# Storing a spectral product channel by channel in a long-convolution kernel

## The chip, the cores and the metric

The kernel runs on one core of a Trainium2 chip. What counts is the device time of one execution in microseconds (us), as the median of several runs. Times below are in us unless marked ns. The engines are PE (TensorE: weight loads and matrix products), DVE (VectorE), ACT (ScalarE), POOL (GpSimd) and SP (SyncE, which here only issues DMAs). Each engine works through its own list of instructions in order.

## The reference

The input is one sequence of 2048 positions with 640 channels. After a layer norm it feeds two branches whose product is added back to the input:

```python
xn = _layernorm(x)
# branch A: a state-space convolution, one long kernel K per channel
P = exp((A * dt)[:, :, None] * pos)              # 640 channels x 128 modes x 2048 positions
K = 2 * einsum("dn,dnl->dl", C, P).real          # 640 kernels of 2048 taps
y = irfft(rfft(u, 2L) * rfft(K, 2L), 2L)[:L]     # causal convolution, plus u * D_skip
# branch B: a router picks 8 tokens for a gated expert; the others pass unchanged
g = silu(B(xn))
return x + s * g
```

## The kernel before

The 640 channels are 160 groups of four, worked on in **five batches of 32 groups** (`SIZES`). A sequence of 2048 positions is seen as 32 x 64, and its transform is done in two steps. For every batch the kernel does this:

1. **Kernel tables.** For four groups at a time PE forms phases (`arg`, L1030), ACT takes sines (L1044), POOL and DVE multiply them with magnitudes (L1007, L1016, L1051 to L1065), and PE sums over the 128 modes (`K`, L1078).
2. **First step of the transform.** Over the 32: `stage1_x` (L1122) transforms the signal, `stage1` (L1113) the kernel. The result has 32 residues for each channel, so a group has 4 x 32 = 128 values m. Their constants are `c[:, C_X...]` and `c[:, C_W...]`, built by `shape_constants()`. ACT and DVE copy the results out of PSUM (helper `copy`, L477) into `g_all` for the signal and `fk` for the kernel. `fk` holds 4096 floats in each partition; rows 0 to 63 belong to groups 0 to 15 of the batch and rows 64 to 127 to groups 16 to 31.
3. **Second step, product.** `dft` (L1151) runs for each of eight values `kp`, two halves each, on signal and kernel at once. `ue` copies one part out of PSUM (L477), `xp` multiplies (DVE, L1170), and `combine` makes the real and the imaginary part of the complex product with one subtraction and one addition (helper `tt`, L480; 34 of the 40 pairs on POOL, 6 on DVE). Its result goes back into `fk`, into the very places that this `kp` has just read.
4. **Inverse of the second step.** `inv` (L1193) runs four times a batch, for q = 0 to 3. Each time PE loads 32 stationary operands of 64 rows by 128 columns out of `fk` and multiplies each with 128 columns of the constants at `C_D`. Loads for rows 0 to 63 and rows 64 to 127 alternate, so 32 products are 16 pairs. One stationary operand is one group: its 128 columns are the 128 values m of that group's real or imaginary part. `inve` copies the result out of PSUM into `gb` (L477, 32 of the 40 copies on ACT, 8 on DVE).
5. **Last step and gate.** L1242 for the first three batches, L1332 for the last two, with the gate, the residual and the stores around them.

In `fk` the product lies as `(q r m g)`: half, real or imaginary, m, and then eight groups side by side. So the 128 columns that one `inv` loads stand **eight floats (32 bytes) apart**.

**What sets the order.** Nothing is decided while the kernel runs. A planner (`Plan`) holds all tasks; a table `ORDER` gives each its rank, and `CHOICE` gives the engine where there is a choice. The code is issued in the order of these ranks, so the tables of the next batch stand between the `inv` tasks of this one: on PE an `arg`, a `K` or a `stage1_x` that stands behind an `inv` cannot start before it. `inv` and most other products take their PSUM from one ring of four slots (`f`); an `inv` takes two. The layout also appears in the planner's bookkeeping: `stage1` for quarter q of `fk` waits for two `inv` tasks (`fkfree`).

Of the kernel before, what the change touches and what calls it, by code (L numbers as in the profile page):

```python
# [15 lines left out]
OP = mybir.AluOpType  # L16
# [125 lines left out]
}  # L142
MODE = {"K": 1, "rt": 1, "ff": 1, "t2m": 1, "s2": 2, "turn": 2, "inv": 3, "arg": 3, "s1x": 2, "s1k": 4, "t1m": 4, "t2g": 5}
CODE = {"K": 136, "s1x": 64, "s1k": 128, "rt": 128, "s2": 32, "inv": 64, "t1m": 64, "t2m": 64, "turn": 32, "ff": 20, "arg": 8, "t2g": 8}
BLOCK, FETCH, SHARE, CAP, SOFT = 254.9, 3.0, 1.0, 4.5, 1.3
SWITCH = 0.135
LETTER = {"PE": "P", "DVE": "D", "ACT": "A", "POOL": "G", "SP": "S"}
# [35 lines left out]
def shape_constants():  # L183
    bm = np.arange(64)
    k1, a, k2 = np.arange(32), np.arange(32), np.arange(64)
    c = np.zeros((128, C_END))
    w = np.zeros((4, 32, 2, 4, 32))
    ph = 2 * np.pi * (((4 * k1[None] + 1) * a[:, None]) % 128) / 128
    for d in range(4):
        w[d, :, 0, d] = np.cos(ph)  # L190
        w[d, :, 1, d] = np.sin(ph)
    c[:, C_X:C_X + 256] = w.transpose(0, 1, 2, 3, 4).reshape(128, 256)
    w = w.reshape(2, 64, 2, 2, 64)
    c[:, C_W:C_W + 128] = np.concatenate([w[0, :, :, 0], w[1, :, :, 1]]).reshape(128, 128)
# [12 lines left out]
    m[0, :, :, 0], m[1, :, :, 0] = np.cos(ph), -np.sin(ph)
    m[0, :, :, 1], m[1, :, :, 1] = np.sin(ph), np.cos(ph)
    l = 64 * a[None] + bm[:, None]
    ph = 2 * np.pi * (((4 * k1[:, None, None] + 1) * l[None]) % 8192) / 8192  # L210
    v = np.stack([np.cos(ph), np.sin(ph)], 2) / 2048.0
    v = np.broadcast_to(v[None], (4, 32, 64, 2, 32)).reshape(128, 64, 2, 32)

    pos = np.zeros((3, 2, 32))
    pos[0, 1], pos[1, 0], pos[2, 0] = (a + 0.5) / TURN, a / TURN, 1.0 / TURN
    p = np.zeros((4, 32, 2, 2, 4, 32))
    for q in range(4):
        for x in range(2):  # L220
# [194 lines left out]
def kernel(ctx: ExitStack, tc: tile.TileContext, xq, xp, xr, par, ldtp, dsk, wr, wg, wu, wd,  # L415
# [571 lines left out]
    def kernel(gg):  # L987
# [103 lines left out]
        if odd:  # L1091
            P.add(KEVAC, lambda e: copy(e, kb.t.rearrange("p e b -> p (e b)"), kp.t), [kp], [("kb", gg)], [kb], kind="kb")
            p, q = (Slot("f"), Slot("f")), (gg % 8) // 2
            free = [("fkfree", 2 * (q // 2) + z) for z in range(2)]
            on("PE", S1K, lambda: stage1(p, lambda e: kb.t[:, e]),
               [kb, ("kb", gg), "c"] + free, new=p, kind="s1k")
            for h in range(2):
                P.add(EVAC, lambda e, h=h: copy(e, fk[:, 1024 * q + 512 * h:1024 * q + 512 * h + 512].rearrange("p (m c) -> p m c", c=8),
                                                p[h].t.rearrange("p (c m) -> p m c", c=8)),
                      [p[h]] + free, [("fk", batch(gg), q, h)], kind="s1ke")  # L1100
# [41 lines left out]

    def dft(o, bi, kp, j):

        u = g_all[:, 4 * bi:4 * bi + 4].rearrange("p (s q) (d k i g) -> p s i k (q d) g", s=2, d=4, k=8, i=4)
        for e in range(2):
            for ri in range(2):
                for h in range(2):
# [2 lines left out]
                    T.matmul(o[64 * h:64 * h + 64, :, ri, e], ms[kp].t[:, 2 * j + e, 64 * ri:64 * ri + 64], v, start=True, stop=True,  # L1151
                             tile_position=(0, 64 * h))

    def transform(bi):
        udep = [("g", gg, h) for gg in range(STARTS[bi] // 4, (STARTS[bi] + NG) // 4) if gg % 2 == 0 for h in range(2)]
        kdep = [("fk", bi, q, h) for q in range(4) for h in range(2)]
        for kp in range(8):
            pq = Slot("pq")
            for j in range(2):
                p = Slot("f")  # L1160
                on("PE", S2, lambda p=p, kp=kp, j=j: dft(p.t.rearrange("p (a r x e g) -> p a r e x g", a=2, r=2, x=8, e=2), bi, kp, j),
                   [ms[kp]] + udep + kdep, [("S2", bi, kp, j)], [p], kind="s2", mac=.853)
# [11 lines left out]
                on("DVE", .62, product, [p, pq, ("u", bi, kp, j)], [("xp", bi, kp, j)], kind="xp")  # L1174

            def combine(e, pq=pq, kp=kp):
                z = fk.rearrange("p (q r d k x) -> p k r q d x", r=2, q=2, d=4, k=8)[:, kp]
                v = lambda k, u: pq.t[:, k, u].rearrange("p (q d x) -> p q d x", q=2, d=4)
                tt(e, z[:, 0], v(0, 0), v(1, 1), OP.subtract)
                tt(e, z[:, 1], v(1, 0), v(0, 1), OP.add)  # L1180

# [2 lines left out]
        for q in range(4):  # L1184
            p = Slot("f"), Slot("f")

            def inv(p=p, q=q):
                fz = fk.rearrange("p (q r m g) -> p r q g m", r=2, q=2, g=8)
                for j in range(4):
                    for ri in range(2):  # L1190
                        for h in range(2):
                            r = slice(64 * h, 64 * h + 64)
                            T.matmul(p[h].t[:, 128 * j:128 * j + 128], fz[r, ri, q // 2, 4 * (q % 2) + j],  # L1193
                                     c[r, C_D + 128 * ri:C_D + 128 * ri + 128], start=(ri == 0), stop=(ri == 1),
                                     tile_position=(64 * h, 0))
# [232 lines left out]
```

## Time and profile before

| | us |
|---|---|
| median of 3 runs (441.22 to 441.88) | 441.74 |
| the profiled execution | 442.32 |
| its span, first to last instruction | 440.4 |
| PE busy | 361.3 |
| DVE busy | 343.5 |
| POOL busy | 280.9 |
| ACT busy | 267.8 |
| mean granted PE clock | 0.961 |

"PE" is time in matrix products and "PEld" time in weight loads; the two overlap. A group of instructions is written as line, engine, operation, output<-input, shapes and count, then busy time and mean ns of one, then the idle time of the engine just before them and what ended it. Shapes of PE instructions begin with rows*columns of the stationary operand. The chain is the sequence of work that ended last, followed back from the last instruction; `154.00 3.80 PE f L1193 x32` means that from 154.00 on 32 instructions of line 1193 held the chain for 3.80 us. A timeline row has start, length, engine, line, operation and count, and in brackets how long the engine stood idle before and for what. A row of stages gives busy time and instruction count of PE, PEld, DVE, ACT and POOL in a stretch, then the PE clock, the DMA share and GB/s.

### The profile page before, as it was taken

What the parts mean: (1) busy time and instruction counts of PE and PEld (TensorE: products, weight loads), DVE (VectorE), ACT (ScalarE), POOL (GpSimd) and SP (SyncE); (2) the same over time, 40 slices, a digit from 0 to 9 for tenths busy, and PEclk for the clock granted to TensorE, in tenths of its full rate; (3) what the DMA queues carried; (4) which work ended last, traced back from release to release, by engine and by line L of the source; (5) the groups of instructions that cost most, each with busy time, mean ns of one, the idle gap of its engine ahead of it and who ended that gap; (6) DMA issues with size and microseconds to landing.
All of it is one profiled execution on the core that took longest, in us unless ns stands there. A gap on an engine that the chain in (4) does not pass through costs nothing.

```text
span 440.4 us, 19524 instructions
## 1 busy us (share of the span) xinstructions
PE 361.3 (82%) x8634; PEld 313.3 (71%) x8634; DVE 343.5 (78%) x665; ACT 267.8 (61%) x508; POOL 280.9 (64%) x345
## 2 busy tenths in 40 slices
PE   1066367866699996989899999999889899989995
PEld 1055356634477884867788899997688789889995
DVE  3787798999878947789977778558979987788255
ACT  3994936687648457567735486559866856541010
POOL 0558991655367858659653579738998974968200
PEclk9996859989999999999997999999999999999999
DMA  7915332649344411312101000303455651168704
GB/s 244 365 29 101 96 119 70 213 155 247 119 147 166 133 52 56 102 51 76 52 1 40 3 3 3 104 2 124 151 184 169 217 176 60 54 162 190 226 25 170
DMA packets 41596, 51.30 MB, mean 116 GB/s; under 512 B 19560, under 2 KB 30632, under 8 KB 41384
## 3 DMA queue, kind: packets, MB, share of 16 engines
q1 hardware_dynamic: 40200, 48.17, 36.0%
q10 hardware_dynamic: 1152, 1.84, 1.1%
q8 instruction: 68, 1.11, 1.0%
q14 instruction: 16, 0.13, 0.1%
q0 software_dynamic: 160, 0.04, 0.0%
HBM read 44.75 MB, written 10.52 MB: 125 GB/s over the span
## 4 chain that ended last, share of the span: by engine, by line
PE 45%; DVE 13%; ACT 5%; issue 3%; DMA 1%; POOL 1%; ACTq 0%; DVEq 0%; SPq 0%
PE f L1193 18%; PE f L1151 10%; DVE tab L1051 4%; PE f L1078 4%; PE f L1332 3%; PE f L1122 2%; PE pr L1030 2%; DVE both L1170 2%; PE f L1113 2%; ACT pr L1044 2%; ACT both L477 2%; PE f L1242 1%; DVE both L480 1%; DMA wflat<-cw 1%; DVE tab L1060 1%
## 5 line engine op out<-in xcount | busy, mean ns | idle before, releaser
L477 ACT COPY both<-f 128x512 f32<-128x512 f32 (+1 forms) x142 | 69.3, 511 | 100.4 <-PE f L1193 56.1
L1051 DVE TENSOR_TENSOR tab<-pr,ma 128x1024 f32<-128x1024 f32 x80 | 97.2, 1218 | 24.5 <-ACT pr L1044 15.3
L1007 POOL TENSOR_TENSOR ma<-ma,et 128x64 f32<-128x64 f32 (+4 forms) x100 | 89.6, 896 | 22.2 <-ACT ma L477 9.0
L1044 ACT ACTIVATE pr<-pr 128x1024 f32<-128x1024 f32 x80 | 80.4, 1014 | 30.3 <-PE pr L1030 28.2
L1193 PE MATMUL f<-c,both 64*128 64x128 f32 x640 | 80.4, 404 | 1.3 <-ACT both L477 1.1
L1193 PEld LDWEIGHTS f<-c,both 64*128 64x128 f32 x640 | 78.0, 331 | 3.0 <-issue 1.3
L1151 PE MATMUL f<-both 128*64 128x128 f32 x1280 | 76.3, 275 | 4.0 <-DVE both L1170 1.6
L1151 PEld LDWEIGHTS f<-both 128*64 128x64 f32 x1280 | 69.7, 137 | 10.5 <-DVE both L1170 3.9
L1065 POOL TENSOR_TENSOR tab<-tab,ma 128x256 f32<-128x256 f32 x48 | 34.9, 749 | 46.2 <-DVE tab L1051 44.6
L480 POOL TENSOR_TENSOR both<-both 128x256 f32<-128x256 f32 (+1 forms) x69 | 49.9, 748 | 15.6 <-DVE both L1170 12.6
L1170 DVE TENSOR_TENSOR both<-both,f 128x512 f32<-128x512 f32 x80 | 52.8, 683 | 3.9 <-ACT both L477 2.9
L477 DVE COPY both<-f 128x512 f32<-128x512 f32 (+1 forms) x58 | 32.1, 557 | 28.5 <-PE f L1193 20.6
L1078 PE MATMUL f<-tab 128*32 128x64 f32 x2560 | 45.6, 223 | 6.5 <-ACT both L477 2.4
L1078 PEld LDWEIGHTS f<-tab 128*32 128x32 f32 x2560 | 39.0, 111 | 16.0 <-issue 6.9
L1122 PE MATMUL f<-c,both 128*64 128x128 f32 x640 | 41.1, 282 | 2.4 <-ACT both L477 1.3
L1122 PEld LDWEIGHTS f<-c,both 128*64 128x64 f32 x640 | 36.3, 140 | 5.8 <-ACT both L477 2.2
L1016 POOL TENSOR_TENSOR ma<-ma,et 128x1024 f32<-128x1024 f32 x20 | 38.8, 1941 | 1.6
L1030 PE MATMUL pr<-pos,st 64*128 64x256 f16 x320 | 30.2, 282 | 10.2 <-DVE tab L1058 5.1
L1030 PEld LDWEIGHTS <-st 64*128 64x128 f16 x320 | 13.3, 101 | 22.0 <-issue 10.1
L1113 PE MATMUL f<-c,kb 64*64 64x64 f32 x1280 | 24.2, 221 | 4.1 <-issue 1.4
L1060 DVE SCALAR_TENSOR_TENSOR tab<-pr,ma 128x512 f32<-128x512 f32 x40 | 27.2, 679 | 0.0
L1113 PEld LDWEIGHTS f<-c,kb 64*64 64x64 f32 x1280 | 21.3, 134 | 7.8 <-issue 2.8
(170 smaller groups left out, 510.6 us busy)
## 6 DMA issues: line engine op xcount, KB each, us to landing
both<-xq SPq DMA_DIRECT2D x8, 640.0 KB
wflat<-wg SPq DMA_DIRECT2D x10, 432.0 KB
wflat<-wu SPq DMA_DIRECT2D x10, 432.0 KB
wflat<-wd SPq DMA_DIRECT2D x16, 270.0 KB
wflat<-cw SPq DMA_DIRECT2D x16, 256.0 KB
xg_d<-xp SPq DMA_DIRECT2D x4, 768.0 KB
wflat<-xg_d SPq DMA_DIRECT2D x16, 192.0 KB
ios<-xp SPq DMA_DIRECT2D x16, 192.0 KB
```

The lines of the kernel that those rows point to most:

```text
L477: {"ACT": S.copy, "DVE": V.tensor_copy, "POOL": G.tensor_copy}[e](out, in_)
L480: {"DVE": V, "POOL": G}[e].tensor_tensor(out, a, b, op=op)
L1007: G.tensor_tensor(both_at(m, 32 - 2 * w, w, w), both_at(m, 32 - w, 0, w), e()[:, q::6].unsqueeze(3).broadcast_to([128, 2, 32, w]), op=OP.mult)
L1030: T.matmul(o.t[:, j].rearrange("p (t h m) -> p h t m", t=2, h=2)[:, h], st.t[64 * j:64 * j + 64, 2 * (gg % 8) + h], pos[64 * j:64 * j + 64 ...
L1044: on("ACT", .93, lambda src=src: S.activation(src.t, src.t, AF.Sin, scale=-TWO_PI), [], [src], table="TS", kind="sin")
L1051: V.tensor_tensor(o, src.t.rearrange("p j (t x) -> p j t x", t=2), m, op=OP.mult)
L1078: T.matmul(o[32 * d4:32 * d4 + 32, dl, :], tab[i].t[:, 0, cc, :], tab[i].t[:, 1:3, cc], start=(not odd and dl + i == 0), stop=False, tile_ ...
L1113: T.matmul(p[h].t[64 * ri:64 * ri + 64, 64 * e:64 * e + 64], src(e)[64 * h:64 * h + 64], c[64 * h:64 * h + 64, w:w + 64], start=True, stop ...
L1122: T.matmul(p[e // 4].t[64 * ri:64 * ri + 64, 128 * (e % 4):128 * (e % 4) + 128], g_all[:, g0 // 8, 64 * e:64 * e + 64], c[:, C_X + 128 * r ...
L1151: T.matmul(o[64 * h:64 * h + 64, :, ri, e], ms[kp].t[:, 2 * j + e, 64 * ri:64 * ri + 64], v, start=True, stop=True, tile_position=(0, 64 * h))
L1170: V.tensor_tensor(bass.AP(tensor=o.tensor, offset=o.offset, ap=[o.ap[0], [512, 2], [32, 16], [1, 16]]), bass.AP(tensor=o.tensor, offset=o. ...
L1193: T.matmul(p[h].t[:, 128 * j:128 * j + 128], fz[r, ri, q // 2, 4 * (q % 2) + j], c[r, C_D + 128 * ri:C_D + 128 * ri + 128], start=(ri == 0 ...
```

## The change

The 32 columns of the first step's constants are permuted: the column that held residue 4k+i at place 4k+i now stands at place 8i+k. The second step finds each `kp` under the new index; its moving operand still has runs of eight floats 256 floats apart, at another offset.

With that, the eight floats that one `kp` writes back at each place are (i, real or imaginary) of **one** group and no longer eight groups. `combine` writes its result as `(g x k i r)`: m and, inside it, real and imaginary part, so that one group (the program's words "channel by channel") fills 256 consecutive floats and a stationary operand of `inv` takes every second one (8 bytes apart). To do so `combine` walks over 4 x 8 x 8 elements, reading runs of eight floats; the elements of its innermost loop go to places 512 floats (2 KB) apart. Before, it wrote runs of 32 floats.

Each `inv` then reads one quarter of `fk` (4q to 4q+3), so `stage1` is listed behind one `inv` in place of two. `inve` writes pairs of floats where it wrote runs of four; it reads the same PSUM addresses in the same order.

The list `APART` is empty, so the new functions `dft1`, `in_u`, `spectrum` and `second` are never called, and the loop in `transform` runs as before. Compared row by row, all five engines issue as many instructions as before, of the same operations and in the same order. PE's and SP's rows are equal. Only the shapes of `combine` (128x2x4x32 becomes 128x4x8x8) and `inve` (128x128x4 becomes 128x128x2x2) differ, and two ACT copies of `stage1` results no longer wait for POOL.

```diff
@@ shape_constants
+    w = w[..., np.arange(32).reshape(8, 4).T.ravel()]
-    c[:, C_X:C_X + 256] = w.transpose(0, 1, 2, 3, 4).reshape(128, 256)
+    c[:, C_X:C_X + 256] = w.reshape(128, 256)
...
@@ kernel
-            free = [("fkfree", 2 * (q // 2) + z) for z in range(2)]
+            free = [("fkfree", q)]
...
@@ dft
-        u = g_all[:, 4 * bi:4 * bi + 4].rearrange("p (s q) (d k i g) -> p s i k (q d) g", s=2, d=4, k=8, i=4)
+        u = g_all[:, 4 * bi:4 * bi + 4].rearrange("p (s q) (d i k g) -> p s i k (q d) g", s=2, d=4, k=8, i=4)
...
@@ transform, combine
-                z = fk.rearrange("p (q r d k x) -> p k r q d x", r=2, q=2, d=4, k=8)[:, kp]
-                v = lambda k, u: pq.t[:, k, u].rearrange("p (q d x) -> p q d x", q=2, d=4)
+                z = fk.rearrange("p (g x k i r) -> p k r i x g", g=8, x=8, k=8, r=2)[:, kp]
+                v = lambda k, u: pq.t[:, k, u].rearrange("p (x i g) -> p i x g", x=8, i=4)
...
@@ transform, inv
-                fz = fk.rearrange("p (q r m g) -> p r q g m", r=2, q=2, g=8)
+                fz = fk.rearrange("p (h m r) -> p h m r", h=HALF, r=2)
...
-                            T.matmul(p[h].t[:, 128 * j:128 * j + 128], fz[r, ri, q // 2, 4 * (q % 2) + j],
+                            T.matmul(p[h].t[:, 128 * j:128 * j + 128], fz[r, 4 * q + 2 * (j % 2) + j // 2, :, ri],
...
@@ transform, inve
-                g = HALF * h + 4 * q
-                P.add(EVAC, lambda e, p=p[h], g=g: copy(
-                    e, gb[:, bi].rearrange("p (m g) -> p m g", g=NG)[:, :, g:g + 4], p.t.rearrange("p (g m) -> p m g", g=4)),
+                P.add(EVAC, lambda e, p=p[h], q=q, h=h: copy(
+                    e, gb[:, bi].rearrange("p (m s u g) -> p s m u g", s=2, u=2, g=8)[:, h, :, :, 2 * q:2 * q + 2],
+                    p.t.rearrange("p (u g m) -> p m u g", u=2, g=2)),
```

More of the change, by code (lines that the diff above doesn't have):

```diff
@@ L142 @@
 }
-MODE = {"K": 1, "rt": 1, "ff": 1, "t2m": 1, "s2": 2, "turn": 2, "inv": 3, "arg": 3, "s1x": 2, "s1k": 4, "t1m": 4, "t2g": 5}
-CODE = {"K": 136, "s1x": 64, "s1k": 128, "rt": 128, "s2": 32, "inv": 64, "t1m": 64, "t2m": 64, "turn": 32, "ff": 20, "arg": 8, "t2g": 8}
+MODE = {"K": 1, "rt": 1, "ff": 1, "t2m": 1, "s2": 2, "s2u": 2, "s2k": 2, "turn": 2, "inv": 3, "arg": 3, "s1x": 2, "s1k": 4, "t1m": 4, "t2g": 5}
+CODE = {"K": 136, "s1x": 64, "s1k": 128, "rt": 128, "s2": 32, "s2u": 64, "s2k": 64, "inv": 64, "t1m": 64, "t2m": 64, "turn": 32, "ff": 20, "arg": 8, "t2g": 8}
 BLOCK, FETCH, SHARE, CAP, SOFT = 254.9, 3.0, 1.0, 4.5, 1.3
@@ L161 @@
 S2 = .93
+APART = []
 S1K, S1X = 1.1, 1.9
@@ L1152, in dft, with dft1, in_u, spectrum @@
                              tile_position=(0, 64 * h))
+    def dft1(p, bi, kp, src):
+        o = p.t.rearrange("p (r x i g) -> p r i x g", r=2, x=8, i=4)
+        v = src.rearrange("p (s q) (d i k g) -> p s i k (q d) g", s=2, d=4, k=8, i=4)
+        for e in range(4):
+            for ri in range(2):
+                for h in range(2):
+                    T.matmul(o[64 * h:64 * h + 64, ri, e], ms[kp].t[:, e, 64 * ri:64 * ri + 64], v[:, h, e, kp], start=True, stop=True,
+                             tile_position=(0, 64 * h))
+    def in_u(bi, kp):
+        return g_all[:, 4 * bi:4 * bi + 4].rearrange("p q (x k g) -> p k (q x) g", x=16, k=8)[:, kp]
+    def spectrum(bi):
+        udep = [("g", gg, h) for gg in range(STARTS[bi] // 4, (STARTS[bi] + NG) // 4) if gg % 2 == 0 for h in range(2)]
+        for kp in range(8):
+            p = Slot("f")
+            P.chain(("u", kp), on("PE", 1.0, lambda p=p, kp=kp: dft1(p, bi, kp, g_all[:, 4 * bi:4 * bi + 4]),
+                                  [ms[kp]] + udep, [("U", bi, kp)], [p], kind="s2u", mac=.853), 8 * STEP)
+            P.add(EVAC, lambda e, p=p, kp=kp: copy(e, in_u(bi, kp), p.t.rearrange("p (x g) -> p x g", g=8)),
+                  [p] + udep, [("X", bi, kp)], kind="s2ue")
+    def second(bi, kp, pq, kdep):
+        p = Slot("f")
+        on("PE", .95, lambda: dft1(p, bi, kp, fk.rearrange("p (q y) -> p q y", q=4)), [ms[kp]] + kdep, [("S2", bi, kp, j) for j in range(2)],
+           [p], kind="s2k", mac=.853)
+        def product():
+            u, v = in_u(bi, kp), p.t
+            V.tensor_tensor(pq.t.rearrange("p k u x -> p (k u x)"),
+                            bass.AP(tensor=u.tensor, offset=u.offset, ap=[u.ap[0], [0, 2], list(u.ap[1]), list(u.ap[2])]),
+                            bass.AP(tensor=v.tensor, offset=v.offset, ap=[v.ap[0], [256, 2], [0, 2], [1, 256]]), op=OP.mult)
+        on("DVE", 1.135, product, [p, ("X", bi, kp)], [("xp", bi, kp, j) for j in range(2)], [pq], kind="xp")
     def transform(bi):
@@ L1158, in transform @@
             pq = Slot("pq")
-            for j in range(2):
+            if bi in APART:
+                second(bi, kp, pq, kdep)
+            for j in range(2 * (bi not in APART)):
                 p = Slot("f")
@@ L1377 @@
         P.chain(("s", gg % 8), stage1_x(gg), 8 * STEP)
+        if gg % 8 == 6 and batch(gg) in APART:
+            spectrum(batch(gg))
     for bi in range(NBATCH):
```

## The prediction

> **What bounds the kernel now.** First the page: who is busy, and who holds the chain that ended last.
>
> ```profile
> PE 361.3 (82%) x8634; PEld 313.3 (71%) x8634; DVE 343.5 (78%) x665; ACT 267.8 (61%) x508; POOL 280.9 (64%) x345
> ...
> PE 45%; DVE 13%; ACT 5%; issue 3%; DMA 1%; POOL 1%; ACTq 0%; DVEq 0%; SPq 0%
> PE f L1193 18%; PE f L1151 10%; DVE tab L1051 4%; PE f L1078 4%; PE f L1332 3%; PE f L1122 2%; PE pr L1030 2%; DVE both L1170 2%; PE f L1113 2%; ACT pr L1044 2%; ACT both L477 2%; PE f L1242 1%; DVE both L480 1%; DMA wflat<-cw 1%; DVE tab L1060 1%
> ```
>
> PE leads, but DVE is close behind. One line stands out: the inverse, L1193, holds 18% of the chain. Then the chain in order of time, which tells whether that is a few long waits or every `inv`:
>
> ```profile
> 154.00 3.80 PE f L1193 x32
> ...
> 227.15 4.21 PE f L1193 x32
> ...
> 253.49 1.90 PE f L1122 x32
> ...
> 410.34 15.43 PE f L1193 x128
> ```
>
> All 20 `inv` tasks are on it, 3.8 us each at full clock (4.2 at 227, in a stage whose mean clock is 0.90, row below). Between them stands the yardstick: L1122 also makes 32 products in 16 pairs, also streams 128 columns and also fills the array, but needs **1.90**. The groups say what differs:
>
> ```profile
> L1193 PE MATMUL f<-c,both 64*128 64x128 f32 x640 | 80.4, 404 | 1.3 <-ACT both L477 1.1
> L1193 PEld LDWEIGHTS f<-c,both 64*128 64x128 f32 x640 | 78.0, 331 | 3.0 <-issue 1.3 <-ACT both L477 1.1
> ...
> L1122 PE MATMUL f<-c,both 128*64 128x128 f32 x640 | 41.1, 282 | 2.4 <-ACT both L477 1.3 <-ACT st L477 0.8 <-DVE both L812 0.2
> L1122 PEld LDWEIGHTS f<-c,both 128*64 128x64 f32 x640 | 36.3, 140 | 5.8 <-ACT both L477 2.2 <-issue 1.3 <-ACT st L477 1.1
> ```
>
> In L1193 weight loads are under way 78.0 of 80.4 us. A load there has 128 columns in place of 64, so twice the work, but 331 ns is more than twice 140. For a load of 128 columns that stand side by side there is the layer norm's sum over constants:
>
> ```profile
> 30.56 0.52 PEld L781 LDWEIGHTS f<-wflat,c 128*128 128x128 f32 x4 [3.02 <-ACT wflat L775]
> L781 PEld LDWEIGHTS f<-wflat,c x8: 186/240/333, 30.6 to 33.0; 128*128 128x128 f32 x8
> ```
>
> Four loads there end 0.52 after the first began, the last of them taking about 0.19: they start (0.52 - 0.19) / 3 = **0.11** apart. In L1193 a pair of loads, which run side by side on the two halves of the rows, comes every 15.43 / 64 = **0.241**. So 128 columns cost 0.11 side by side and 0.241 at 32 bytes apart, and the products need no more than 1.90 / 16 = 0.119 a pair. The inverse waits for its weight loads, and the loads for the spacing.
>
> **The change part by part.**
>
> *Weight loads 8 bytes apart.* No row has this spacing. Bounds: the loads stay at 0.241 (`inv` 3.8, no gain), or they fall to or below the pace of the products (0.119, `inv` 1.90). I take 0.120. Why: at 32 bytes every column is fetched by itself, 0.241 / 128 = 1.9 ns each, against 0.11 / 128 = 0.86 side by side. If a fetch brings a block of 16 bytes or more, two columns or more now share one, and 128 columns need at most 0.241 / 2 = 0.120. An `inv` then takes 16 x 0.120 = 1.92, **1.89 less** than 3.81; twenty of them 37.8.
>
> [...]
>
> *How much of 37.8 reaches the end.* Behind an `inv` PE's list holds `arg` (L1030) and `K` (L1078), for which ACT's sines and DVE's tables wait. What comes earlier by a faster `inv` is their work, so the next bound is DVE. The stages with `inv`, and for comparison the one where DVE rules:
>
> ```profile
> 154.00:164.00 10.00, 10.00 (x150) 9.02 (x148) 4.14 (x6) 5.52 (x8) 6.41 (x6) 1.00 0.19 58
> 179.00:189.00 10.00, 9.95 (x144) 8.89 (x142) 5.83 (x12) 4.58 (x8) 7.75 (x8) 1.00 0.19 58
> 189.00:227.00 38.00, 33.20 (x826) 26.98 (x824) 36.73 (x66) 25.70 (x49) 27.10 (x33) 1.00 0.17 52
> 227.00:262.00 35.00, 33.89 (x746) 31.08 (x748) 25.16 (x48) 19.80 (x35) 18.46 (x21) 0.90 0.05 15
> 278.00:296.00 18.00, 18.00 (x239) 17.46 (x231) 9.86 (x12) 7.97 (x12) 10.45 (x13) 1.00 0.18 59
> 356.00:382.00 26.00, 26.00 (x563) 23.96 (x558) 20.07 (x24) 15.70 (x29) 18.17 (x20) 1.00 0.34 102
> 410.00:426.00 16.00, 16.00 (x152) 15.68 (x146) 5.35 (x9) 1.91 (x4) 0.00 (x0) 1.00 0.36 122
> ```
>
> PE is full in each `inv` stage and nobody else is. From 189 to 227 DVE reaches 36.73 / 38 = 97%, so I let a stage shrink until DVE is at 97%: 154 and 179 can give 3.8 each, 227 gives 7.6 (DVE's floor is 25.16 / 0.97 = 25.9 of 35), 278 gives 7.6 (floor 10.2 of 18), 356 only 26 - 20.07 / 0.97 = **5.3**, the tail at 410 gives 7.6. Together 35.7.
>
> Some is lost where the chain changes hands. In the first batch:
>
> ```profile
> 159.89 1.23 DVE L1051 TENSOR_TENSOR tab<-pr,ma 128x1024 f32<-128x1024 f32 x1 [2.98 <-ACT pr L1044]
> 161.03 0.68 DVE L1060 SCALAR_TENSOR_TENSOR tab<-pr,ma 128x512 f32<-128x512 f32 x1
> 163.92 1.22 DVE L1051 TENSOR_TENSOR tab<-pr,ma 128x1024 f32<-128x1024 f32 x1 [2.21 <-PE f L1078]
> 162.77 1.10 PE L1078 MATMUL f<-tab 128*32 128x64 f32 x64
> ```
>
> Two faster `inv` would let `K` start 3.8 earlier, at 159.0. But its tables end at 161.7, and their sines come only one `inv` (1.9) earlier: 159.8. So 0.8 is lost here. I charge 0.6 in each of the four middle batches, **2.4**. In the tail nothing but the copies out of PSUM stands between the four `inv`; two copies on two engines (591 and 686 ns, rows below) fit into 1.92.
>
> *`combine` writes scattered floats.*
>
> ```profile
> L480 POOL TENSOR_TENSOR both<-both 128x256 f32<-128x256 f32 x68 | 48.6, 740 | 15.6 <-DVE both L1170 12.6 <-ACT both L722 1.6 <-ACT both L477 1.4
> L480 DVE TENSOR_TENSOR both<-both 128x256 f32<-128x256 f32 x12 | 10.6, 922 | 0.1
> L1007 POOL TENSOR_TENSOR ma<-ma,et 128x64 f32<-128x64 f32 x20 | 7.3, 367 | 16.1 <-ACT ma L477 9.0 <-DVE ma L477 6.5
> L1007 POOL TENSOR_TENSOR ma<-ma,et 128x128 f32<-128x128 f32 x20 | 8.7, 433 | 2.1 <-ACT et L725 0.7
> L1007 POOL TENSOR_TENSOR ma<-ma,et 128x256 f32<-128x256 f32 x20 | 12.9, 643 | 1.6
> ACT both L477 <- POOL both L480: 13.4, 14, 1.7
> 389.47 14.40 PE f L1151 x256
> ```
>
> The nearest scattered write is L1007: its form with 64 elements handles single floats 32 apart, the larger ones runs of 2 and 4. From 128 to 256 elements it grows by 210 / 128 = 1.64 ns each, which would put 64 at 328; it takes 367, so single floats cost 39 / 64 = 0.6 ns more. For 256 that is 0.16. Bounds for a POOL operation: 0.74 (no cost) to 0.90; below 0.74 nothing speaks for. The cover is PE: eight `kp` take 14.40 / 8 = 1.80 each, a POOL pair 1.48, at worst 1.80. The copies that already wait for POOL (13.4 us) are where it would show. I take a third of the bound, 0.05 each, and charge 0.2 a batch: **1.0**. The 12 operations on DVE have no scattered row; a doubling would add 11 us to DVE, half of it perhaps on the path, and that goes into the range.
>
> [...] No row here shows a step of 2 KB.
>
> *`inve` writes pairs of floats.*
>
> ```profile
> L477 ACT COPY both<-f 128x512 f32<-128x512 f32 x90 | 50.6, 591 | 73.0 <-PE f L1193 56.1 <-PE f L1122 10.5 <-PE f L1113 6.3
> L477 DVE COPY both<-f 128x512 f32<-128x512 f32 x30 | 20.4, 686 | 25.4 <-PE f L1193 20.6 <-PE f L1113 2.9 <-PE f L1122 1.9
> L477 ACT COPY kb<-f 128x512 f32<-128x512 f32 x15 | 8.9, 591 | 3.2 <-PE f L1083 2.8 <-PE f L1113 0.4
> ```
>
> Runs of four (most of the first kind) cost ACT what a wholly contiguous copy costs (the third row), 591; I charge pairs nothing. ACT's 56 us of waiting for the inverse hide even a doubling; without that cover the last copy of the tail would add 0.6.
>
> *The rest costs nothing.* The permuted constants are as large as before; `dft` streams runs of eight floats as before; the shorter wait list moves no instruction, since the ranks are fixed.
>
> **Sum.** 35.7 - 2.4 - 1.0 = 32.3 off the profiled execution's 442.32 gives 410.0. That execution lay 0.58 above the median, so **409.4**.
>
> **The rivals.**
>
> *A. The loads come only part of the way*, or DVE's chains take more of the gain than the hand-over above. For it: only the two ends of the spacing have rows, and DVE is at 78% already. Against it: the tail and the stage at 278 have DVE half idle. With loads at 0.18 an `inv` takes 2.9, the 20 give 18, and with the same share lost (32.3 of 37.8 arrive) about 16 remain: **426**.
>
> *B. Nothing changes.* The loads would have to be slow for another reason than the spacing, say the two halves of the rows loading at once. For it: the contiguous row loads all 128 rows in one piece. Against it: L1113 and L1242 load 64 rows, too, and take no longer for 64 columns than L1122 with its 128 rows (140):
>
> ```profile
> L1113 PEld LDWEIGHTS f<-c,kb 64*64 64x64 f32 x1280 | 21.3, 134 | 7.8 <-issue 2.8 <-ACT both L477 2.6 <-DVE ios L638 1.0
> L1242 PEld LDWEIGHTS f<-both,wflat 64*64 64x64 f32 x512 | 11.5, 133 | 3.3 <-issue 2.5 <-DVE both L1170 0.7
> ```
>
> With the 1.0 of `combine`: **442.2**, within 0.2%. [...]
>
> *C. Slower, by `combine` on POOL.* In the second step each `kp` needs its pair before PSUM and product buffers come free. The point from which it decides is a pair of 1.80, an operation of 0.90; each 0.1 us beyond adds 34 x 0.1 = 3.4 us for the 34 pairs on POOL. To eat all 33 a pair must reach 2.8, an operation 1.4, or 1.9 times today's. For it: the inner step goes from 1 float to 512. Against it: the scattered row costs 0.6 ns an element, which just reaches 0.90. At 1.5 an operation (34 x 1.2 = 41 us, against the 33 gained): **450**.
>
> **How the numbers follow.** Chances: forecast 0.75, A 0.15, B 0.04, C 0.06. The forecast's own range is 401 to 420: all 37.8 and the 3 by which L1193's 18% of the span, 79 us, exceeds 20 x 3.81 = 76 (some `inv` run at a lower clock) give 401; two thirds of the sum give 420. To leave out no more than two in ten it needs a little of A: **401 to 423**. What this kernel's measurement can tell from no change is about 0.2%, 0.9 us. Faster: forecast and A, and a little of C where POOL takes only a part, **0.92**. Same: **0.03**, most of B. Slower: **0.05**.
>
> **What would show it.** L1193's loads near 230 ns or less and their pieces near 1.9 in the chain confirm the loads; 3.8 says B, 2.9 says A. Faster loads with a time above 420 mean that the gain was lost on the way: then DVE's idle time in the `inv` stages has not shrunk, or new waits for L480 appear. A POOL row of L480 above 900 ns is C. [...] I am wrong if the 0.120 is.

## The result, and the profile after

The changed kernel takes **406.59 us** (median of 4 runs, 406.36 to 408.85) against 441.77 for the kernel before on the same chip (4 runs, 441.22 to 441.88): **0.9217** times the time before, 95% interval 0.9184 to 0.9251, or 35.2 us less. 409.4 was predicted, with a range of 401 to 423. The profiled execution took 406.41, its span 404.5. Lone executions far above the rest (771.19 and 628.60 of the kernel before, 1628.86 of one below) are left out of ranges and ratios here, the last one also of its median. Line numbers have moved: `inv` is now L1233 (before L1193), `dft` L1153 (L1151), `combine` L482 (L480), the copies L479 (L477), `xp` L1210 (L1170).

The page of the changed kernel, busy time and then the chain by engine and by line:

```profile
PE 322.8 (80%) x8634; PEld 274.7 (68%) x8634; DVE 343.9 (85%) x665; ACT 268.3 (66%) x508; POOL 281.6 (70%) x345
...
PE 35%; DVE 33%; ACT 14%; issue 7%; POOL 6%; DMA 4%; SPq 0%; ACTq 0%; DVEq 0%; POOLq 0%
PE f L1153 11%; DVE tab L1053 10%; PE f L1233 5%; PE f L1080 4%; PE f L1372 4%; DVE both L1210 3%; DVE tab L1062 3%; PE f L1115 3%; ACT both L829 3%; ACT pr L1046 2%; DVE both L1295 2%; PE pr L1032 2%; PE f L1124 2%; ACT both L810 2%; ACT both L479 2%
```

The inverse fell from 18% of the chain to 5%, and DVE's tables (L1053) rose from 4% to 10%. DVE is now the busiest engine, with as much work as before (343.9 against 343.5). The chain in order of time:

```profile
151.44 1.89 PE f L1233 x32
154.79 1.88 PE f L1233 x32
...
221.68 2.20 PE f L1233 x32
...
382.13 7.74 PE f L1233 x128
```

An `inv` takes 1.9 where it took 3.8 (in batch 1, 2.1 to 2.2 where it took 4.0 to 4.2), and the four of the tail take 7.74 where they took 15.43. The groups of the same line, and the yardstick:

```profile
L1233 PE MATMUL f<-c,both 64*128 64x128 f32 x640 | 41.8, 281 | 1.4 <-ACT both L479 1.2
L1124 PE MATMUL f<-c,both 128*64 128x128 f32 x640 | 39.4, 275 | 3.6 <-ACT both L479 1.5
L1233 PEld LDWEIGHTS f<-c,both 64*128 64x128 f32 x640 | 39.4, 193 | 3.2 <-issue 1.3
```

A weight load has gone from 331 ns to 193, and the same 640 products take 41.8 us in place of 80.4, near the 39.4 of the products that always had close loads.

Where the 440.4 - 404.5 = 35.9 us of span went is read from five stages, each from the start of a batch's first `inv` to the end of its fourth. The kernel before (length of the stretch after its bounds, then PE, PEld, DVE, ACT, POOL, the clock, DMA share, GB/s):

```profile
153.84:188.58 34.74, 29.74 (x684) 25.09 (x682) 22.42 (x36) 20.62 (x32) 23.90 (x26) 1.00 0.22 67
227.15:252.42 25.27, 24.59 (x444) 22.49 (x448) 18.82 (x37) 11.34 (x17) 11.25 (x13) 0.86 0.06 19
278.49:295.74 17.25, 17.25 (x212) 16.92 (x208) 9.53 (x11) 7.55 (x11) 10.24 (x13) 1.00 0.15 51
356.70:381.51 24.81, 24.81 (x494) 22.89 (x496) 18.94 (x22) 14.59 (x26) 17.05 (x18) 1.00 0.35 106
410.27:425.78 15.51, 15.51 (x134) 15.39 (x136) 5.16 (x8) 1.76 (x3) 0.00 (x0) 1.00 0.35 121
```

The same stages of the changed kernel:

```profile
151.28:180.13 28.85, 23.82 (x684) 18.19 (x682) 22.36 (x36) 20.64 (x32) 20.87 (x25) 0.94 0.26 78
218.82:236.08 17.26, 16.41 (x444) 14.61 (x448) 16.63 (x34) 11.42 (x17) 11.26 (x13) 1.00 0.09 26
262.16:271.81 9.65, 9.65 (x212) 9.27 (x208) 8.03 (x10) 7.63 (x11) 7.97 (x10) 1.00 0.29 93
332.57:352.36 19.79, 17.97 (x494) 15.41 (x496) 17.96 (x21) 14.84 (x26) 15.71 (x16) 1.00 0.43 133
382.06:389.87 7.81, 7.81 (x134) 7.69 (x136) 5.17 (x8) 1.82 (x3) 0.00 (x0) 1.00 0.72 242
```

| | predicted gain | measured gain |
|---|---|---|
| batch 0 | 7.6 - 0.6 = 7.0 | 34.74 - 28.85 = 5.9 |
| batch 1 | 7.6 - 0.6 = 7.0 | 25.27 - 17.26 = 8.0 |
| batch 2 | 7.6 - 0.6 = 7.0 | 17.25 - 9.65 = 7.6 |
| batch 3 | 5.3 - 0.6 = 4.7 | 24.81 - 19.79 = 5.0 |
| tail | 7.6 | 15.51 - 7.81 = 7.7 |
| between these stages and behind the tail | -1.0 | -0.9 |
| before the first `inv` | 0 | 153.84 - 151.28 = 2.6 |

From the first `inv` on, 33.3 us were gained, against 32.3 predicted. The 2.6 before it lie where the kernel is nearly the same; over the kernels below, the first `inv` starts between 150.7 and 153.6 where loads are close and between 152.3 and 154.2 where they are not, on average at 152.2 and 153.2, so more than half of the 2.6 belongs to the execution and not to the change. A second measurement of the same kernel (below) gave 33.0 in all. The stages vary between executions, too: in the one profiled there they are 29.3, 17.3, 9.7, 21.3 and 8.1 long, so batch 3 gained 3.5 and not 5.0.

### The profile page after: what moved, and what is told of

Same layout as the page of the kernel before. It is cut to its first block, busy times and chain, and to the rows that moved or that the text cites. A ratio compares the mean times of both kernels' runs of the same rounds, so it can differ in the third digit from the quotient of the medians.

```text
span 404.5 us, 19522 instructions
## 1 busy us (share of the span) xinstructions
PE 322.8 (80%) x8634; PEld 274.7 (68%) x8634; DVE 343.9 (85%) x665; ACT 268.3 (66%) x508; POOL 281.6 (70%) x345
## 3 DMA queue, kind: packets, MB, share of 16 engines
q10 hardware_dynamic: 1152, 1.84, 1.2%
## 4 chain that ended last, share of the span: by engine, by line
PE 35%; DVE 33%; ACT 14%; issue 7%; POOL 6%; DMA 4%; SPq 0%; ACTq 0%; DVEq 0%; POOLq 0%
PE f L1153 11%; DVE tab L1053 10%; PE f L1233 5%; PE f L1080 4%; PE f L1372 4%; DVE both L1210 3%; DVE tab L1062 3%; PE f L1115 3%; ACT both L829 3%; ACT pr L1046 2%; DVE both L1295 2%; PE pr L1032 2%; PE f L1124 2%; ACT both L810 2%; ACT both L479 2%
## 5 line engine op out<-in xcount | busy, mean ns | idle before, releaser
L479 ACT COPY both<-f 128x512 f32<-128x512 f32 (+1 forms) x142 | 69.9, 515 | 66.9 <-PE f L1233 24.0
L1053 DVE TENSOR_TENSOR tab<-pr,ma 128x1024 f32<-128x1024 f32 x80 | 97.2, 1217 | 12.1 <-ACT pr L1046 8.3
L1153 PE MATMUL f<-both 128*64 128x128 f32 x1280 | 76.6, 275 | 4.3 <-DVE both L1210 1.7
L1153 PEld LDWEIGHTS f<-both 128*64 128x64 f32 x1280 | 69.9, 137 | 11.0 <-DVE both L1210 4.1
L482 POOL TENSOR_TENSOR both<-both 128x256 f32<-128x256 f32 (+1 forms) x69 | 50.2, 755 | 14.4 <-DVE both L1210 11.7
L1210 DVE TENSOR_TENSOR both<-both,f 128x512 f32<-128x512 f32 x80 | 52.7, 682 | 4.1 <-ACT both L479 3.1
L1080 PE MATMUL f<-tab 128*32 128x64 f32 x2560 | 46.7, 226 | 6.6 <-ACT both L479 2.4
L1080 PEld LDWEIGHTS f<-tab 128*32 128x32 f32 x2560 | 40.1, 114 | 15.9 <-issue 4.5
L1233 PE MATMUL f<-c,both 64*128 64x128 f32 x640 | 41.8, 281 | 1.4 <-ACT both L479 1.2
L1124 PE MATMUL f<-c,both 128*64 128x128 f32 x640 | 39.4, 275 | 3.6 <-ACT both L479 1.5
L1233 PEld LDWEIGHTS f<-c,both 64*128 64x128 f32 x640 | 39.4, 193 | 3.2 <-issue 1.3
L479 DVE COPY both<-f 128x512 f32<-128x512 f32 (+1 forms) x58 | 32.1, 556 | 8.7 <-PE f L1115 2.9
L1124 PEld LDWEIGHTS f<-c,both 128*64 128x64 f32 x640 | 34.8, 136 | 6.9 <-ACT both L479 2.3
```

The lines of the kernel that those rows point to most:

```text
L479: {"ACT": S.copy, "DVE": V.tensor_copy, "POOL": G.tensor_copy}[e](out, in_)
L482: {"DVE": V, "POOL": G}[e].tensor_tensor(out, a, b, op=op)
L1053: V.tensor_tensor(o, src.t.rearrange("p j (t x) -> p j t x", t=2), m, op=OP.mult)
L1080: T.matmul(o[32 * d4:32 * d4 + 32, dl, :], tab[i].t[:, 0, cc, :], tab[i].t[:, 1:3, cc], start=(not odd and dl + i == 0), stop=False, tile_ ...
L1124: T.matmul(p[e // 4].t[64 * ri:64 * ri + 64, 128 * (e % 4):128 * (e % 4) + 128], g_all[:, g0 // 8, 64 * e:64 * e + 64], c[:, C_X + 128 * r ...
L1210: V.tensor_tensor(bass.AP(tensor=o.tensor, offset=o.offset, ap=[o.ap[0], [512, 2], [32, 16], [1, 16]]), bass.AP(tensor=o.tensor, offset=o. ...
```

## Experiments

### What the loads are worth, and which spacing decides

Four kernels change the operand of `inv` alone; the new expressions are written short here. **The loads alone**, in the kernel before: old `combine`, old `inve`, but stationary columns two floats apart.

```diff
-                fz = fk.rearrange("p (q r m g) -> p r q g m", r=2, q=2, g=8)
...
-                                     fz[r, ri, q // 2, 4 * (q % 2) + j],
+                                     fk[r, 1024*q + 256*j + ri:1024*q + 256*j + ri + 255:2],
```

> The kernel before, with one edit: the 128 columns of each stationary operand of the inverse are taken two floats apart out of the same quarter of fk. The product is stored as before, so the inverse multiplies other numbers than it should and the result is not the reference's; the amount of work is the same. Theory (the spacing of the loads is all that counts): loads 193 ns, a task of the inverse 1.9 us, and a time like the changed kernel's 406.6, at most 1.0 us below it, which is what the prediction charged for scattered writes of combine. Rival (the other parts of the change carry some of the gain, or cost more than charged): above 408, or below 405.

**The changed kernel with its loads put back** to eight floats apart:

```diff
-                                     fz[r, 4 * q + 2 * (j % 2) + j // 2, :, ri],
+                                     fk[r, 1024*q + 2*j + ri:1024*q + 2*j + ri + 1017:8],
```

> The changed kernel, with one edit: the inverse takes its columns eight floats apart again (out of the same quarter of fk; wrong numbers, same work). Theory: loads 331 ns, 0.241 us a pair, 3.8 us a task, and the time of the kernel before, 441 to 443. Rival (the gain came from storing the product by group, from the shorter wait list or from the quarter being read as a whole): near 407. Rival B of the prediction (spacing does not matter to a load): 331 ns would not come back.

The changed kernel with columns **four floats apart** (16 bytes), and with columns **side by side**:

```diff
+  four apart:   fk[r, 1024*q + 2*(j % 2) + ri + 512*(j // 2):1024*q + 2*(j % 2) + ri + 512*(j // 2) + 509:4],
+  side by side: fk[r, 1024*q + 128*(2*j + ri):1024*q + 128*(2*j + ri) + 128:1],
```

> The changed kernel, columns of the inverse four floats (16 bytes) apart (wrong numbers, same work). If a fetch brings 16 bytes: one column a fetch, as at eight floats, 0.241 us a pair and 441 us. If it brings 32 bytes: two columns share one, 0.120 a pair and 407. If the price grows evenly with the step: about 0.16 a pair, 2.6 us a task, near 419.

> The changed kernel, columns of the inverse side by side (wrong numbers, same work). Theory: loads at most 0.11 us a pair, so the products set the pace, 0.119 a pair as in the first step: 1.90 us a task and 406.2 to 406.6, no measurable gain over two floats apart. Rival (at two floats apart the load still holds the products up a little): a task nearer 1.75 us, and 2 to 3 us less, 404.

Measured, all against the same runs of the kernel before (440.99):

| kernel | us (range, runs) | ratio, 95% interval |
|---|---|---|
| before with close loads | 408.78 (403.87 to 413.19, 6) | 0.928, 0.924 to 0.933 |
| changed, 32 bytes apart | 442.20 (439.82 to 444.91, 10) | 1.003, 1.000 to 1.006 |
| changed, 16 bytes apart | 441.35 (439.81 to 443.98, 10) | 1.003, 1.000 to 1.006 |
| changed, 4 bytes apart | 406.89 (405.18 to 408.69, 4) | 0.923, 0.919 to 0.927 |

The groups of the first and of the second:

```profile
L1192 PEld LDWEIGHTS f<-c,both 64*128 64x128 f32 x640 | 40.1, 193 | 4.0 <-issue 2.4 <-ACT wflat L1230 0.7 <-ACT both L477 0.3
```

```profile
L1232 PE MATMUL f<-c,both 64*128 64x128 f32 x640 | 80.8, 404 | 1.7 <-ACT both L479 1.1 <-issue 0.4
L1232 PEld LDWEIGHTS f<-c,both 64*128 64x128 f32 x640 | 78.2, 331 | 3.6 <-issue 1.8 <-ACT both L479 1.1 <-POOL both L482 0.2
```

One line brings nearly the whole gain into the kernel before (32.2 of the 33.0 to 35.2 us), and one line takes it out of the changed kernel, with 193 and 331 ns a load. The 408.78 of the first lies just above the 408 from which its expectation spoke of a rival. That rival is not shown by it: the changed kernel, measured again, took 408.26, the profiled execution of the close loads 403.87, and without its two slowest executions their median is 407.37. Rival B (nothing changes, because the loads are slow for the halves of the rows) has fallen: halves and columns are the same in all four. At 16 bytes everything is as slow as at 32, so the step lies between 8 and 16 bytes. Side by side brings nothing beyond 8 bytes that the time shows, though a pair comes a little faster (112 ns in place of 118, table below).

### Between 8 and 32 bytes

If a load pays for each block of 16 bytes that it touches, columns 12 bytes apart touch 96 blocks for 128 columns and must lie in between, while 24 bytes must cost as much as 32.

```diff
+  12 bytes: fk[r, 1024*q + j % 3 + 384*ri:1024*q + j % 3 + 384*ri + 382:3],
+  24 bytes: fk[r, 1024*q + (2*j + ri) % 6:1024*q + (2*j + ri) % 6 + 763:6],
```

> The changed kernel, columns of the inverse three floats (12 bytes) apart (wrong numbers, same work). Four and eight floats both took 0.233 to 0.238 us a pair, so one column a fetch already at 16 bytes. Theory (the price is the number of 16-byte blocks touched, 1.86 ns each, never faster than the products): three floats touch 96 blocks for 128 columns, 0.18 a pair, 2.9 us a task, near 425. Rival (it jumps: full speed up to two floats, else one price for each column): 0.238 a pair and 441. Rival (any two columns that follow each other in one block are enough): 0.12 a pair and 407.

> The changed kernel, columns six floats (24 bytes) apart (wrong numbers, same work). Theory: every column has its own 16-byte block, 0.238 us a pair and 441. Rival (blocks of 32 bytes, which four floats already speak against): 0.18 a pair and 425.

The kernel with 12 bytes took 424.16 (423.25 to 424.94; ratio 0.962, 0.952 to 0.972), the one with 24 bytes 436.25 (one execution); the kernel before took 439.77 on that chip. Their loads, 12 bytes and then 24:

```profile
L1232 PEld LDWEIGHTS f<-c,both 64*128 64x128 f32 x640 | 57.7, 258 | 3.1 <-issue 1.3 <-ACT both L479 1.2 <-POOL both L482 0.2
```

```profile
L1232 PEld LDWEIGHTS f<-c,both 64*128 64x128 f32 x640 | 73.4, 313 | 3.4 <-issue 1.8 <-ACT both L479 1.2
```

All spacings together; a pair is the median distance from one pair of products to the next, the tail is the stretch with its four `inv`:

| bytes apart | blocks of 16 bytes touched | one load, ns | a pair, ns | tail, us |
|---|---|---|---|---|
| 4 | 32 | 192 | 112 | 7.65 |
| 8 | 64 | 193 | 118 | 7.81 |
| 12 | 96 | 258 | 174 | 11.42 |
| 16 | 128 | 325 | 233 | 15.20 |
| 24 | 128 | 313 | 223 | 14.55 |
| 32 | 128 | 331 | 238 | 15.51 |

238 / 128 = 1.86 ns a block gives 119 for 64 blocks (118 measured), 179 for 96 (174) and would give 60 for 32, where 112 was measured: there something else sets the pace, perhaps the products, whose pairs in the first step (L1124, the yardstick) come every 109. At 8 bytes the two limits lie only 9 ns apart. So from 8 bytes on the rows agree with a price by blocks touched, within 6%; a price in proportion to the spacing up to 16 bytes would give the same numbers, and these spacings do not tell the two apart. That 24 bytes are 6% cheaper than 32 (223 against 238) is explained by neither, and stays open. The 441 expected for 24 bytes was not met either.

### What `combine` may cost

Rival C said that `combine` decides the time once a POOL pair takes more than 1.80. The changed kernel's pairs do not. So one kernel makes them dear: the two inner loops are exchanged, so that the results lie 8 bytes apart, but the operands are read 32 bytes apart. Another keeps all runs of eight floats, in reading and writing, with the operands in one piece. Of both, only the access patterns are shown.

```diff
-                v = lambda k, u: pq.t[:, k, u].rearrange("p (x i g) -> p i x g", x=8, i=4)
+  loops exchanged: z "... -> p k r g x i",  v "p (x i g) -> p g x i"
+  runs of eight:   z "p (n k y) -> p k n y",  v "p (n y) -> p n y"
```

> The changed kernel, with combine's loops turned round: its innermost loop now runs over i (results two floats apart in one block of eight floats, inputs eight floats apart) and no longer over the group (results 512 floats apart, inputs side by side). The same numbers at the same places. The changed kernel's rows: POOL 746 ns, DVE at least 586 where the kernel before had 412. If DVE pays for scattered results, DVE falls back to 412; if it pays for short loops or for inputs that are not side by side, it stays at 586 or rises. [...] Time: 405 to 407 with POOL at 746, 413 with POOL at 1000.

> The changed kernel, with combine writing runs of eight floats from inputs that are read side by side in one piece (the numbers land at other places than the inverse expects, so the result is wrong; the amount of work is the same). If it is the scattered results that cost DVE its 586 in place of 412, it falls back to 412; POOL stays at 740. Time 405 to 408.

The group of `combine` on POOL in the changed kernel, and ACT's wait for it (us, times, longest):

```profile
L482 POOL TENSOR_TENSOR both<-both 128x256 f32<-128x256 f32 x68 | 48.8, 746 | 14.4 <-DVE both L1210 11.7 <-ACT both L724 1.6 <-ACT both L479 1.0
L482 DVE TENSOR_TENSOR both<-both 128x256 f32<-128x256 f32 x12 | 12.2, 1094 | 0.1
```

```profile
ACT both L479 <- POOL both L482: 13.3, 14, 1.7
```

The same with the loops exchanged:

```profile
L482 POOL TENSOR_TENSOR both<-both 128x256 f32<-128x256 f32 x68 | 76.2, 1157 | 5.8 <-DVE both L1210 3.8 <-ACT both L724 1.6
```

```profile
ACT both L479 <- POOL both L482: 23.9, 16, 2.7
```

Loops exchanged, the kernel took 418.36 (417.17 to 418.71; ratio 0.948, 0.941 to 0.956). That is 418.36 - 406.59 = 11.8 us more than the changed kernel, and more than the 413 expected with POOL at 1000 ns, a figure that no run shows: POOL took 1157. A POOL pair now takes 2 x 1.157 = 2.31, and by C's formula 34 x (2.31 - 1.80) = 17 should be lost. So the mechanism of C is real, and its formula is somewhat too dear; the added wait on ACT, 23.9 - 13.3 = 10.6, is the better measure. The changed kernel itself stays clear of it: 746 ns an operation against 740 before, and ACT waits 13.3 against 13.4.

The exchange alters three things at once: operands 32 bytes apart, results 8 bytes apart, and an innermost loop of four in place of eight. Runs of four alone do not make POOL slow, since L1007 takes 643 ns for 256 elements with them (row in the prediction); operands and results were not tried one by one. DVE's shortest operation did not fall back to 412, as it should if only results far apart cost it something: it took 610, and the 12 operations of 256 elements took 1259 ns on average where they took 1094.

With runs of eight, POOL took 737 ns and the kernel 408.94 (one execution). The shortest `combine` on DVE fell back to 412 ns from 586. To see whether reading or writing costs DVE that, a third kernel reads as the changed kernel does and writes runs of eight.

```diff
-                z = fk.rearrange("p (g x k i r) -> p k r i x g", g=8, x=8, k=8, r=2)[:, kp]
+                z = fk.rearrange("p (r i x k y) -> p k r i x y", r=2, i=4, x=8, k=8)[:, kp]
```

> The changed kernel, with combine reading its inputs as it does there (runs of eight, in another order than they lie) but writing runs of eight floats 64 apart (the numbers land at other places than the inverse expects; wrong result, same work). The shortest DVE operation was 412 ns with both in long runs, 586 in the changed kernel. If results 512 floats apart cost DVE the difference: 412 here. If the reading in short runs does: 586.

It took 408.28 (one execution). The rows of `combine` on DVE (shortest, median and longest, in ns; the forms of 256 and 512 elements share the row), changed kernel first, then this one:

```profile
L482 DVE TENSOR_TENSOR both<-both x19: 586/691/2256, 126.5 to 400.8; 128x256 f32<-128x256 f32 x12, 128x512 f32<-128x512 f32 x7
```

```profile
L482 DVE TENSOR_TENSOR both<-both x19: 411/684/2134, 128.1 to 402.6; 128x256 f32<-128x256 f32 x12, 128x512 f32<-128x512 f32 x7
```

Between these two kernels only the places of the results differ, so in the changed kernel it is the results 2 KB apart that cost DVE 0.17 us an operation, 2 us of busy time for the 12; none of it can be seen in the time. The 610 of the exchanged loops says that this is not the only access that costs DVE so much.

### Is DVE the next bound?

The prediction let a stage shrink until DVE is 97% busy. If DVE's work sets the pace, moving some of it to ACT should make the kernel faster, as long as ACT has room where the work goes. One kernel moves the five DVE copies of `inve` in batches 0 to 3 to ACT, a second one moves ten copies of stage 1 as well, and the changed kernel is measured again beside them.

```diff
-    "inve.0": "AAAAAADA", "inve.1": "DAADAAAA", "inve.2": "AAAAAAAD", "inve.3": "AAAAAADA", "inve.4": "DAAADAAD",
+    "inve.0": "AAAAAAAA", "inve.1": "AAAAAAAA", "inve.2": "AAAAAAAA", "inve.3": "AAAAAAAA", "inve.4": "DAAADAAD",
...  second kernel only
-    "s1ke.0": "DAADAAAA", "s1ke.1": "AAAAAAAA", "s1ke.2": "ADDAADDA", "s1ke.3": "DAAAADDD",
+    "s1ke.0": "AAAAAAAA", "s1ke.1": "AAAAAAAA", "s1ke.2": "AAAAAAAA", "s1ke.3": "AAAAAAAA",
```

> The changed kernel itself, as the yardstick for the two runs beside it, which differ by a few us at most: 404 to 409.

> The changed kernel, with the five copies out of the inverse's PSUM that DVE makes in the first four batches given to ACT (0.69 us each, 3.4 us off DVE; ACT has 66 per cent busy time, DVE 85). Same result. Theory (after the change DVE is what the stages with inv wait for): 1 to 3 us faster than the changed kernel beside it. Rival (PE's order and the handing over between engines set the pace, DVE's share alone does not): no difference, or up to 1 us slower, since both copies of one inv then stand behind each other on ACT.

> As the run before, and also the ten copies of the kernel's first step that DVE makes in the first four batches on ACT (15 copies, 10 us off DVE, 9 us onto ACT). Same result. Theory (DVE): 3 to 6 us faster than the changed kernel. Rival (handing over): no gain, or slower by some of the 0.6 us that a second copy on the same engine comes later, ten times.

Against the same runs of the kernel before (441.29): the changed kernel 408.26 (406.31 to 410.67; ratio 0.925, 0.920 to 0.929), five copies moved 411.95 (410.21 to 412.92; 0.932, 0.928 to 0.936), fifteen moved **423.77** (422.46 to 427.17; 0.961, 0.957 to 0.966). Less work on DVE made it slower, by 3.7 and 15.5 us, which is more than either side of the two expectations had allowed. Batch 1's stage shows how. PE in the kernel with five copies moved (in brackets PE's idle time before and what ended it), and then the stretch around it by engines:

```profile
225.10 0.50 PE L1233 MATMUL f<-c,both 64*128 64x128 f32 x2 [0.29 <-ACT both L479]
227.44 3.78 PE L1233 MATMUL f<-c,both 64*128 64x128 f32 x30 [1.84 <-ACT both L479]
```

```profile
222.25:244.47 22.22, 19.46 (x444) 17.34 (x448) 15.51 (x32) 12.40 (x19) 11.25 (x13) 0.85 0.07 21
227.00:234.00 7.00, 6.56 (x150) 6.32 (x154) 1.39 (x3) 3.01 (x5) 0.00 (x0) 0.54 0.21 60
```

The first of these copies empties a PSUM buffer that the second `inv` needs. On DVE it was done in time; on ACT it stands behind two sines (1.94), PE waits 1.84 longer, and the granted clock in the 7 us from there on is 0.54. Of this `inv` the 30 products behind the wait then take 3.78. So the stage takes 22.2 in place of 17.3, which is the 3.7 and more; the low clock has as large a part in that as the wait. With fifteen moved, the waits of the second step grow, too (13.4 and 11.7 us in the changed kernel), and then PE's row there:

```profile
ACT both L479 <- PE f L1153: 19.5, 19, 6.4
POOL both L482 <- DVE both L1210: 18.9, 15, 9.1
```

```profile
259.49 13.30 PE L1153 MATMUL f<-both 128*64 128x128 f32 x190 [4.60 <-ACT both L479]
```

PE stands idle for 4.60 before its second step, and the stretch from batch 1 to batch 2 takes 33.5 in place of 26.1. So "the busiest engine is the bound" is not enough here: in these stages it matters who stands behind whom at a hand-over. The two kernels load ACT as they relieve DVE, so what DVE's relief alone would bring they do not show. For batch 3, where the prediction used the cap, these kernels tell little: DVE is busy there for 17.99 and 17.76 in place of 17.96, so it was hardly relieved, and the stage stayed at 19.8 and 19.7.

No version beats the changed kernel. The one with columns side by side and the two with runs of eight compute other numbers and are not told apart from it in time.

## Why the prediction was right, point by point

**The loads (20 x 1.89 = 37.8): right, and its reason fits the runs.** 1.92 was taken for an `inv`; the chain shows 1.88 to 1.91 in batch 0 and 1.94 in the tail (2.08 to 2.20 in batch 1), and the busy time of the line fell by 80.4 - 41.8 = 38.6. The argument, 128 columns each fetched alone at 32 bytes and two to a block at 8, agrees with the six spacings: 238 ns a pair at 32 bytes, 118 at 8. That a fetch brings blocks was the author's reading of 0.241 and 0.11; the runs show only the times. The choice of 0.120 rested on a fetch of 16 bytes or more; of these only 16 fits the runs, since at 16 bytes apart nothing is gained (233 ns). Two readings beside it were off. The "0.119 a pair" of the products is a whole task of L1122 over 16 and so contains the end of the last product; the distance of its pairs is 109 ns, so at 8 bytes apart the loads still come a little slower than products can. And the 4.2 of some `inv` in the kernel before is not due to the clock:

```profile
232.02 4.24 PE f L1193 x32
239.19 4.17 PE f L1193 x32
```

The granted clock was 0.50 in the first (232.0 to 236.2) and 1.00 in the second (239.2 to 243.4), and pairs come every 238 in both. The slow loads hid the low clock; the fast ones do not: behind the wait of 1.84 above, where the clock was 0.54 over 7 us, pairs come every 214 in place of 118, and 30 products take 3.78. The range used this reading for its lower end of 401.

**The cap on DVE (35.7 of 37.8): right in size, its reason not shown.** Batch 3 gave 5.0 (3.5 in the second execution), where 5.3 less 0.6 was worked out, and batch 1, where no cap was seen, gave 8.0. In batch 3 DVE is busy for 17.96 of 19.79, 91% and not 97%. What holds PE there (kernel after, PE; then POOL's wait in the same stretch):

```profile
340.16 0.44 PE L1115 MATMUL f<-c,kb 64*64 64x64 f32 x10 [0.75 <-issue]
344.93 1.10 PE L1080 MATMUL f<-tab 128*32 128x64 f32 x64 [0.86 <-POOL tab L1067]
```

```profile
POOL tab L1067 <- DVE tab L1053: 2.9, 2, 2.5
```

Of PE's 19.79 - 17.97 = 1.8 us of idle time there, 0.86 are the chain that was foreseen (DVE's tables, here through POOL's part of them, ahead of `K`), and 0.75 are a gap in which PE waited for nothing that the profile shows. In the kernel before, PE was never idle in this stage. Whether DVE's busy time would cap it stays open.

**The hand-over (2.4): nearly right as a sum, wrong in its place, so the sum is luck.** Before it was charged, the four stages were to give 3 x 7.6 + 5.3 = 28.1; they gave 26.5, so 1.6 was lost. The 0.8 in batch 0 was worked out from `K`, which was to wait for tables that end at 161.7. PE and then DVE there, changed kernel:

```profile
154.62 2.06 PE L1233 MATMUL f<-c,both 64*128 64x128 f32 x32
156.61 1.10 PE L1080 MATMUL f<-tab 128*32 128x64 f32 x64
...
159.34 0.69 PE L1115 MATMUL f<-c,kb 64*64 64x64 f32 x31 [0.64 <-issue]
```

```profile
155.64 1.23 DVE L1053 TENSOR_TENSOR tab<-pr,ma 128x1024 f32<-128x1024 f32 x1 [1.29 <-ACT pr L1046]
156.78 0.68 DVE L1062 SCALAR_TENSOR_TENSOR tab<-pr,ma 128x512 f32<-128x512 f32 x1
```

`K` (L1080) starts at 156.61, as soon as the `inv` ends, while the tables in question are still being made (until 157.46). So it does not need them: the step took the table nearest in time for the one that is needed. What is lost behind it is 0.64 in the middle of `stage1`, again with no releaser. The same gap, 0.26 to 0.91, stands there in all eight other kernels with loads 4 or 8 bytes apart, and in none of the five with slower loads, the kernel before among them. Its cause was not tried.

Batch 0 lost 1.7 of 7.6 in all, and mostly not to waiting: PE is idle there for 34.74 - 29.74 = 5.0 before and 28.85 - 23.82 = 5.0 after, but its clock was 0.94 in place of 1.00. The kernel before with close loads had clock 1.00 in this stage:

```profile
151.07:179.24 28.17, 22.55 (x684) 17.55 (x682) 22.40 (x36) 20.62 (x32) 20.88 (x25) 1.00 0.27 79
```

There the stage gains 34.74 - 28.17 = 6.6, so at equal clock 1.0 is lost, against 0.6 charged. Batch 1 gained 0.4 more than 7.6 while its clock rose from 0.86 to 1.00; since most of the low stretch in the kernel before lay under slow loads, the clock explains that only in part. The forecast's sum has no term for the clock. A clock below 1.00 comes and goes between stages and executions, and that batch 0 fell short by about as much as batch 1 exceeded its forecast is luck, too.

**`combine` (1.0): charged too high on POOL, and too small to be seen.** 746 ns in place of 740 makes 0.4 us over 68 operations, where 0.05 each, 3.4 us, had been taken; DVE's scattered operations, put into the range alone, cost 0.17 each. Two comparisons bound what reaches the time: the changed kernel with its loads put back is 0.3% slower than before (interval 0.0 to 0.6%, so 0 to 2.6 us), and the kernel before with close loads, which has the old `combine`, is no faster than the changed one (0.928 against 0.922 and 0.925). With the loops exchanged, operands 32 bytes apart and results 8 bytes apart, POOL took 1157 ns in place of 746, which is 55% more for the whole operation; since reads and results both moved, no run shows the reads alone.

**`inve` (0): right.** ACT's copies out of the `f` ring, of which `inve` is about a third, take 598 on average in place of 591 (row below): 0.6 us over 90, under 24.0 us of waiting for the inverse.

```profile
L479 ACT COPY both<-f 128x512 f32<-128x512 f32 x90 | 51.2, 598 | 39.6 <-PE f L1233 24.0 <-PE f L1124 8.5 <-PE f L1115 6.9
```

**The rivals.** A (loads at 0.18, 426) has its mechanism, but at another spacing: 12 bytes give 0.174 and 424.16. B fell with the loads put back. C needs pairs above 1.80; here they take 1.49.

## What to carry to other kernels

Look at the spacing of a stationary operand's columns as well as at their number: in fp32, 128 columns cost 118 ns a pair at 8 bytes apart and 223 to 238 at 16 bytes or more, so here two columns to 16 bytes were enough, and going on to side by side brought 6 ns a pair and nothing that the time shows. Here it paid to let an engine with slack scatter its results so that PE can load densely: the scattered stores on POOL cost 6 ns of 746, those on DVE 0.17 us of 0.59. When a stage shortens, read off what the next instruction really needs, and do not take work off the busiest engine before the trace shows who waits for that work: here that cost 4 and 16 us.

## What the runs showed of the hardware

- **The price of a weight load went with the touched blocks of 16 bytes** from 8 bytes apart on: about 1.86 ns a block for a pair of 64-row fp32 loads (118 ns for 64 blocks, 174 for 96, 233 and 238 for 128). For 32 blocks, columns side by side, it was 112 and not 60; there the products may set the pace (their pairs come every 109 in L1124). A price in proportion to the spacing up to 16 bytes would fit as well. The 24-byte spacing is 6% cheaper than that (223 ns) and unexplained.
- **POOL and DVE reacted differently to a scattered operation.** For 256 fp32 elements, results 2 KB apart cost POOL next to nothing (746 against 735 to 740 ns) and DVE 0.17 us (586 against 411). Operands 32 bytes apart with results 8 bytes apart cost POOL 0.41 us (1157), while DVE's shortest was 610, little above its 586; which of the two sides costs POOL that was not separated.
- **A low granted clock did not slow loads 32 bytes apart**: their pairs came every 238 ns at 0.50 as at 1.00, while pairs of loads 8 bytes apart went from 118 to 214 (30 products in 3.78, the clock 0.54 over 7 us).
- **The granted clock was low behind idle time of PE** in the two kernels with moved copies: 0.54 in the 7 us around a wait of 1.84, and a mean of 0.80 over the 13.30 us behind a wait of 4.60:

```profile
259.50:272.80 13.30, 13.30 (x192) 13.13 (x194) 8.60 (x16) 5.12 (x11) 5.63 (x8) 0.80 0.01 1
```

That the wait caused it was not tried, and its length alone does not decide: in batch 1 of the kernel before, 0.50 stood from 229.5 to 236.3 behind a wait of 0.89, and a wait of 0.88 at the same place in the changed kernel was followed by 1.00.
